# Decode attention with 256 MB of K and 256 MB of V on one core: tiles of 4 MB become tiles of 8 MB, and the sums of K's products move from ScalarE to GpSimd and VectorE

## The chip, the core and the metric

The kernel runs on one core of a Trainium2 chip. The core has TensorE (PE, matmuls), VectorE (DVE), ScalarE (ACT), GpSimd (POOL) and SyncE (SP, which here only issues transfers), and 16 DMA engines that move data between the chip's memory and the core's own memory of 128 partitions. The metric is the device time of one execution in microseconds.

## The reference

One decode step for two sequences (B = 2, one new token each, D = 512): a pre-normalised attention block over a cache of 8192 positions with 32 heads of width 128, and then a channel MLP with its own layer norms (F = 1792). All in float32. Cut to what matters:

```python
q = (layernorm(x) @ wq)                      # (2, 512) @ (512, 4096) -> 32 heads of 128
scores = einsum("bhqd,bhkd->bhqk", q, k_cache) * 128 ** -0.5     # k_cache: (2, 32, 8192, 128)
p = softmax(scores)
o = einsum("bhqk,bhkd->bhqd", p, v_cache)
h = x + o.reshape(2, 1, 4096) @ wo           # wo: (4096, 512)
y = layernorm(layernorm(h))
h2 = h + gelu(y @ w1 + b1) @ w2 + b2         # w1: (512, 1792), w2: (1792, 512)
```

k_cache and v_cache are 268 MB each (2 x 32 x 8192 x 128 x 4 bytes), wq and wo 8.4 MB each, w1 and w2 3.7 MB each. Everything is read once.

## The kernel before, in words

**Tiles.** A "pair" in this kernel is one head of one sequence; there are 64, in the order head 0 sequence 0, head 0 sequence 1, head 1 sequence 0, and so on. K of a pair is 8192 x 128 floats, 4 MB, and comes as one transfer into a tile of 128 partitions: partition p holds 64 positions in a row, so each partition receives one run of 32 KB. V comes in the same way. K, V, the two halves of wq, w1 and w2 share one pool of five slots of 4 MB (`kv`, `bufs=BUFS`). SP issues the transfers in the written order: in turn i the loop (L337 to L386) issues K of pair i + 1 and V of pair i - 1 (`load`, L204 to L209). An issue waits on SP until its slot is free, that is until the tile that held the slot has been used up.

**Scores.** q is made once (L175 to L184), kept in `q2`, and spread over all partitions in PSUM for two heads at a time (`make_q`, L188). For each of the two halves of a K tile VectorE multiplies the half by q in place (`multiply`, L217: 32 positions x 128). Then the products are summed over the 128 columns. ScalarE sums 10 of the 32 positions of a half, one instruction each with its accumulator read (`by_act`, L222), and VectorE the other 22 in one reduction (`by_dve`, L226). 

**Softmax.** After both sequences of a head, the maximum over all positions is found (`row_max` on VectorE, two transposes on TensorE, `all_max` on VectorE and a matmul that spreads it), and ScalarE takes the exponentials into a tile `ptz` that is zero elsewhere (`exps`, L250). `total` sums them with a matmul, `inverse` takes the reciprocal.

**Values.** For V, TensorE multiplies four positions per partition at a time (`values`, L271: 16 matmul groups per tile, 128 x 512 each, into `so2`). ScalarE copies the result out (`gather`), TensorE adds the parts (`head_sum`), VectorE scales by the inverse sum (`head_out`).

**wo.** The first 28 heads are multiplied by wo in four groups. Outputs are collected in a row layout `orow`, transposed per group (`turn`), and multiplied with the group's wo tile (`turned`, L326). The first two groups (7 heads each) get their wo through 24 small transfers that GpSimd issues (`load_spread`, L97 to L119), each after the last and with 16 tiny `fill` transfers between them; the other groups and the last four heads are loaded by SP. Most of wo comes in runs of 8 KB.

**Tail.** After the loop SP issues the last V in three pieces, then w1 in four and w2 in six (L388 to L395). The mean over D, the layer norm, w1, GELU and w2 follow (L397 to L494). The result leaves in two transfers of 2 KB, one on SP's queue and one on ScalarE's (L494). b1 and b2 are loaded by SP eight pairs before the end (L351 to L353).

**Order.** A scheduler places the instructions of each engine from the order in which the program writes them; `tc.issue_after` (`behind`, L331) ties a block of instructions behind a given one on the same engine. It also puts in the waits between engines, for reads after writes and for writes after writes, transfers among them.

Of the kernel before, what the change touches and what calls it, by code (L numbers as in the profile page):

```python
# [15 lines left out]
P = 128  # L16
EPS = 1e-5
QG = 2
WG = 8
LH = 4  # L20
UH = 7
SHUT = (0, 32)
CH = 32
NACT = 10
BUFS = 5
NG = 4
WARM = 3


@with_exitstack  # L30
def tile_decode_block(ctx: ExitStack, tc: tile.TileContext, x, k, v, wq, wo, w1, b1, w2, b2, out):
# [4 lines left out]
    NS = SK // P  # L36
    NC = NS // CH
# [3 lines left out]
    SCALE = DH ** -0.5  # L41

    const = ctx.enter_context(tc.tile_pool(name="const", bufs=1))
    wts = ctx.enter_context(tc.tile_pool(name="wts", bufs=1))
    wtl = ctx.enter_context(tc.tile_pool(name="wtl", bufs=1))
    kv = ctx.enter_context(tc.tile_pool(name="kv", bufs=BUFS))
    work = ctx.enter_context(tc.tile_pool(name="work", bufs=3))
# [3 lines left out]

    x2 = const.tile([B, D], F32, name="x2")
    nc.scalar.dma_start(x2, x.rearrange("b s d -> (b s) d"))

    wo_g = {}
    HL = H - LH

    NP7 = P - 8 * len(SHUT)
    groups = [[(0, UH, 0)], [(UH, UH, 0)], [(14, 2, 0), (16, 4, 2)], [(20, 4, 0), (24, 4, 4)]]
    spread_groups = 2
    part_of = {h: (g, pt) for g, parts in enumerate(groups) for pt in parts for h in range(pt[0], pt[0] + pt[1])}
    group_end = {parts[-1][0] + parts[-1][1] - 1: g for g, parts in enumerate(groups)}
    group_rows = [WG if g < spread_groups else sum(pt[1] for pt in parts) for g, parts in enumerate(groups)]

    def load_wo(g):
        t = wts.tile([P, WG, D], F32, name="wog")  # L70
        for h0, n, r0 in groups[g]:
            nc.sync.dma_start(t[:, r0:r0 + n], wo[h0 * DH:(h0 + n) * DH, :].rearrange("(p r) n -> p r n", r=n))
        wo_g[g] = t

    wqv = wq.rearrange("(p r) n -> p r n", r=DC)
    wqs = []
    for r in range(0, DC, 2):
        t = kv.tile([P, 2, H * DH], F32, name="wqs", tag="kv")
        nc.sync.dma_start(t, wqv[:, r:r + 2, :])  # L79
        wqs += [t[:, 0, :], t[:, 1, :]]  # L80
# [3 lines left out]
    orow = const.tile([B, WG, P], F32, name="orow")  # L84
    nc.gpsimd.memset(orow, 0.0)
    fill = const.tile([2, 8, 2, 2], F32, name="fill")
    turns = iter(range(8 * spread_groups))
    pool = [nc.gpsimd.memset(fill, 0.0)]

    def in_turn(dst, src):  # L90
        with tc.issue_after(pool[0].ins):
            pool[0] = nc.gpsimd.dma_start(dst, src)  # L92

    def turn_to(n):
        in_turn(fill[:n, next(turns) % 8, :, 0:1], b1[:8 * n].rearrange("(p x a c) -> p x a c", p=n, x=2, a=2)[:, 0, :, 0:1])

    def load_spread(g, gate):  # L97
        t = wts.tile([P, WG, D], F32, name="wog")
        h0, n, _ = groups[g][0]
        with tc.issue_after(pool[0].ins):  # L100
            pool[0] = nc.gpsimd.tensor_copy(fill[:1, 0, 0, 1:2], gate)
        for p0 in SHUT:
            with tc.issue_after(pool[0].ins):
                pool[0] = nc.gpsimd.memset(t[p0:p0 + 8], 0.0)  # L104
        dst = t.rearrange("p (s r) n -> p s (r n)", s=2)
        src = wo[h0 * DH:(h0 + n) * DH, :].rearrange("(s q r) n -> q s (r n)", s=2, q=NP7)

        def piece(p0, k):
            q0 = p0 - sum(8 for x in SHUT if p0 > x)
            in_turn(dst[p0:p0 + 4 * k - 3:4], src[q0:q0 + 4 * k - 3:4])  # L110

        for j in range(4):
            turn_to(2)
            piece(40 + j, 14)
        for j in range(4):
            turn_to(2)
            piece(8 + j, 6)
            piece(96 + j, 8)
        wo_g[g] = t  # L119
# [319 lines left out]
    with behind(last):  # L439
        head_sum(hl)  # L440
# [80 lines left out]
```

## Time and profile before

| | |
|---|---|
| device time, median of 3 runs (lowest to highest) | 1317.86 us (1317.77 to 1317.9) |
| the profiled execution, first to last instruction | 1316.0 us |
| busy: VectorE, PE, ScalarE, GpSimd | 990.2, 521.9, 442.0, 39.0 us |
| moved by DMA | 561.65 MB, 427 GB/s over the span |
| of it through SP's and ScalarE's queues | 557.35 MB |
| through GpSimd's queue | 3.68 MB |

The runs report a time of their own; no separate total is given for the profiled execution, so its span is what sums are made against, and 1.9 us lie between it and the median of the runs. Lines of a profile read as follows. A group of instructions is "line engine operation output<-input shapes xcount | busy us, mean ns of one | idle time of the engine just before them <-what ended most of it". A stretch is "from:to, its length, busy us of PE, PEld, VectorE, ScalarE and GpSimd with counts, the granted TensorE clock, the share of the DMA engines' time, GB/s". A line in order of time is "start us, duration us, engine, line, operation". SPq and ACTq are the queues on which SP and ScalarE issue transfers; the duration there is that of the issue, not of the transfer. A line of waits is "engine line <- whom it waited for: total us, times, longest us". DMA issues are "what, queue, count, KB each, median us from issue to landing".

### The profile page before, as it was taken

To read this page: it belongs to the slowest core of one execution; us is meant where nothing else is said; L and a number is where in the kernel's file an instruction comes from. 1 tells how busy PE (TensorE), PEld (TensorE's weight loads), DVE (VectorE), ACT (ScalarE), POOL (GpSimd) and SP (SyncE) were. 2 spreads that over 40 slices of the span, in tenths; PEclk is the share of its full clock that TensorE was granted. 3 is DMA by queue.
4 is the path that set the end of the run, shared out by engine and by line. 5 is a ranking of instruction groups with operands and counts; after the bars stand their busy time and mean duration, and the time that the engine had idled before them with its cause. 6 is when DMAs were issued, how large, how long until landed. Compare 5 with 4: busy or idle time off the path is not lost.

```text
span 1316.0 us, 9726 instructions
## 1 busy us (share of the span) xinstructions
PE 521.9 (40%) x2906; PEld 142.2 (11%) x2907; DVE 990.2 (75%) x462; ACT 442.0 (34%) x2763; POOL 39.0 (3%) x58
## 2 busy tenths in 40 slices
PE   3043254234534243243543344262343432345347
PEld 1010011101101010011100001010010100011013
DVE  1998778778868778778768778778678778688771
ACT  0433334324323334334323333323233333243341
POOL 0310000000320000000000000000000000000000
PEclk9565766666776675666756766676666665767669
DMA  9999999999999999999999999999999999999997
GB/s 409 426 432 429 432 431 431 429 432 431 431 426 430 431 433 430 430 430 430 431 430 430 430 431 432 430 430 429 432 429 430 432 432 426 432 430 432 429 426 318
DMA packets 23597, 561.65 MB, mean 427 GB/s; under 512 B 3620, under 2 KB 3636, under 8 KB 5432
## 3 DMA queue, kind: packets, MB, share of 16 engines
q1 hardware_dynamic: 21868, 557.35, 98.8%
q0 software_dynamic: 1664, 3.68, 0.7%
q8 instruction: 23, 0.38, 0.1%
q14 instruction: 30, 0.25, 0.0%
q10 hardware_dynamic: 12, 0.01, 0.0%
HBM read 561.01 MB, written 0.00 MB: 426 GB/s over the span
## 4 chain that ended last, share of the span: by engine, by line
DMA 72%; DVE 20%; PE 6%; issue 1%; ACT 0%; SPq 0%; DVEq 0%
DMA kv<-in_A_k_cache_dram 53%; DMA kv<-in_A_v_cache_dram 15%; DVE kv L217 12%; DVE s L226 7%; PE so L271 4%; DMA w1s<-in_B_w_dram 3%; PE rowacc L326 1%; DMA w2s<-in_B_w_dram 1%; PE qps L192 0%; SPq L208 0%; DVE gm L240 0%; DVE orow L312 0%; ACT kv L222 0%; ACT L250 0%; SPq L79 0%
## 5 line engine op out<-in xcount | busy, mean ns | idle before, releaser
L217 DVE TENSOR_TENSOR kv<-kv,qps 128x4096 f32<-128x4096 f32 x128 | 562.2, 4413 | 275.9 <-DMA kv<-in_A_k_cache_dram 275.9
L222 ACT ACTIVATE kv<-kv 128x128 f32<-128x128 f32 x1280 | 376.0, 295 | 672.9 <-DVE kv L217 657.3
L271 PE MATMUL so<-kv,pt 128*8 128x512 f32 x2048 | 362.1, 847 | 201.9 <-DMA kv<-in_A_v_cache_dram 199.4
L226 DVE TENSOR_REDUCE s<-kv 128x22 f32<-128x2816 f32 x128 | 391.0, 3075 | 0.1
L222 ACT ACTIVATION_READ_ACCUMULATOR kv<-kv 128x1 f32 x1280 | 238.7, 187 | 0.0
L271 PEld LDWEIGHTS so<-kv,pt 128*8 128x8 f32 x2048 | 62.1, 113 | 444.3 <-issue 250.8
L242 PE MATMUL sm<-gm,srow 1*128 1x2 f32 x64 | 18.3, 354 | 193.2 <-DVE gm L240 193.2
L192 PE MATMUL qps<-q,pick 2*128 2x256 f32 x64 | 31.0, 634 | 151.2 <-DVE kv L217 151.2
L278 ACT ACTIVATE ss<-so 128x512 f32<-128x512 f32 x32 | 19.1, 597 | 155.0 <-PE so L271 155.0
L236 PE MATMUL sm<-ident,mx 128*1 128x128 f32 x64 | 17.9, 280 | 110.5 <-DVE mx L233 105.3
L242 PEld LDWEIGHTS sm<-gm,srow 1*128 1x128 f32 x64 | 15.7, 302 | 205.4 <-DVE gm L240 180.4
L259 PE MATMUL sm<-ones,ls 128*2 128x1 f32 x56 | 5.4, 165 | 75.4 <-ACT pt L250 75.4
L192 PEld LDWEIGHTS qps<-q,pick 2*128 2x128 f32 x64 | 17.6, 302 | 157.5 <-DVE kv L217 153.8
L326 PE MATMUL rowacc<-wog,ot 128*2 128x512 f32 x60 | 33.0, 713 | 3.7 <-issue 2.0
L288 PE MATMUL sm<-ss,sel 128*2 128x128 f32 x224 | 29.0, 273 | 13.8 <-ACT ss L278 13.7
L236 PEld LDWEIGHTS sm<-ident,mx 128*1 128x1 f32 x64 | 5.1, 79 | 165.9 <-DVE mx L233 138.3
L250 ACT ACTIVATE pt<-s,nb 128x64 f32<-128x64 f32 x64 | 21.7, 340 | 1.1
L288 PEld LDWEIGHTS sm<-ss,sel 128*2 128x2 f32 x224 | 16.7, 84 | 25.4 <-ACT ss L278 21.3
L233 DVE TENSOR_REDUCE mx<-s 128x1 f32<-128x64 f32 x64 | 14.0, 219 | 6.5 <-ACT kv L222 0.2
L180 PE MATMUL so<-wqs,yT 128*2 128x512 f32 x64 | 10.1, 789 | 11.9 <-DMA wqs<-in_A_wq_dram 11.9
L92 POOL DMA_DIRECT2D wog<-in_A_wo_dram x24 | 13.4, 558 | 40.3 <-DMA wog<-in_A_wo_dram 26.2
L104 POOL MEMSET wog<- 8x4096 f32 x4 | 14.0, 3502 | 5.4 <-PE rowacc L326 5.3
(91 smaller groups left out, 134.0 us busy)
## 6 DMA issues: line engine op xcount, KB each, us to landing
kv<-in_A_k_cache_dram SPq DMA_DIRECT2D x63, 4096.0 KB, 42.4
kv<-in_A_v_cache_dram SPq DMA_DIRECT2D x62, 4096.0 KB, 33.8
wqs<-in_A_wq_dram SPq DMA_DIRECT2D x2, 4096.0 KB, 12.0
kv<-in_A_v_cache_dram SPq DMA_DIRECT2D x3, 2048.0 KB
kv<-in_A_k_cache_dram SPq DMA_DIRECT2D x2, 2048.0 KB, 42.6
w1s<-in_B_w_dram SPq DMA_DIRECT2D x4, 896.0 KB, 33.8
wog<-in_A_wo_dram SPq DMA_DIRECT2D x3, 1024.0 KB, 39.6
w2s<-in_B_w_dram SPq DMA_DIRECT2D x2, 1024.0 KB
```

Source lines behind the costliest of these rows:

```text
L104: pool[0] = nc.gpsimd.memset(t[p0:p0 + 8], 0.0)
L192: nc.tensor.matmul(t[:, b], pick[32 * n:32 * n + B, b, :], q2[32 * n:32 * n + B, at:at + QG * DH], start=True, stop=True)
L217: return nc.vector.tensor_tensor(kc, kc, qb, op=ALU.mult)
L222: nc.scalar.activation(kt[:, j, :], kt[:, j, :], AF.Copy, accum_out=s[:, j:j + 1])
L226: nc.vector.tensor_reduce(ST[i][:, a:e], kt[:, a:e, :], axis=AX.X, op=ALU.add)
L236: nc.tensor.transpose(MT[h][:, e, :], MX[h][:, e:e + 1], ident)
L242: nc.tensor.matmul(GM[h], srow, gm, start=True, stop=True)
L250: nc.scalar.activation(ptz[h % 2][b][:, :, 4 * b:4 * b + 4], s.rearrange("p (u j) -> p u j", j=4), AF.Exp, bias=nb[:, b:b + 1], scale=SCAL ...
L271: m = nc.tensor.matmul(so[32 * n:32 * n + 4 * B], ptz[h % 2][b][:, u, :], vt[:, 4 * u:4 * u + 4, :], start=(b == 0 and u < NG), stop=(b == ...
L278: nc.scalar.activation(SS[h], so2[h % 2], AF.Copy)
L288: nc.tensor.matmul(OP[h], sel[:, :, j], sj, start=(j == 0), stop=(j == 3))
L326: nc.tensor.matmul(rowacc, t[:, r, :], wo_g[g][:, r, :], start=(g == 0 and r == 0), stop=False)
```

## The change

- **Tiles of 8 MB.** For heads 0 to 29, two heads of one sequence are loaded as one tile: head 2g in partitions 0 to 63, head 2g + 1 in partitions 64 to 127, 128 positions per partition, one run of 64 KB each. That makes 30 units (15 pairs of heads x 2 sequences). Heads 30 and 31 are a unit each, with both sequences in one tile, as two transfers (the last V as four) in runs of 32 KB or less. wq is one transfer of 8 MB. The pool has three slots of 64 KB per partition instead of five of 32. In turn i, V of unit i - 1 is issued first and K of unit i + 1 after it.
- **Sums.** A K tile has four parts of 32 positions. VectorE multiplies each. For the first three GpSimd adds the upper 64 columns of the products onto the lower 64 (`halve`), and VectorE sums 64 columns; the fourth it sums whole. ScalarE sums none. VectorE's written order is product 0, product 1, sum 0, product 2, sum 1, product 3, sum 2, sum 3.
- **One softmax per two heads.** Maxima, exponentials (four ScalarE instructions on 64 partitions each), totals, inverses, `values` and `gather` are done once per pair of heads and both sequences.
- **wo by pairs.** One transfer of 512 KB in runs of 4 KB per pair of heads, on SP; one for heads 30 and 31. `load_spread`, its `fill` transfers and all of GpSimd's DMAs are gone.
- **Small transfers.** In the eighth last unit 15 transfers of 1 to 15 short rows each are written into one unused tile `mark`, on SP, each over the one before. b1 and b2 are loaded after the last V, into the slot that w1 and w2 also take.
- **One store.** The result rows stand 16 partitions apart and leave in one transfer on SP. For this the last matmuls are 32 columns wide instead of 2.

```diff
-CH = 32
-NACT = 10
-BUFS = 5
+CH = 32
+NCH = 4
 NG = 4
+LH = 2
+MARKS = 15
...
+    heads = [(2 * g, 2 * g + 1) for g in range(NP)] + [(h, h) for h in range(HL, H)]
+    units = [(g, b) for g in range(NP) for b in range(B)] + [(g, None) for g in range(NP, NP + LH)]
...
-    kv = ctx.enter_context(tc.tile_pool(name="kv", bufs=BUFS))
+    wts = ctx.enter_context(tc.tile_pool(name="wts", bufs=2))
+    kv = ctx.enter_context(tc.tile_pool(name="kv", bufs=3))
...
+    def slot():
+        return kv.tile([P, ROW], F32, name="kv", tag="kv")
...
+    wqt = slot()
+    nc.sync.dma_start(wqt, wq.rearrange("(p r) n -> p (r n)", r=DC))
...
+    def load(src, i, parts):
+        g, b = units[i]
+        h = heads[g][0]
+        t = slot()
+        if b is not None:
+            nc.sync.dma_start(t, src[b, h:h + 2].rearrange("h (p j) d -> (h p) (j d)", j=NS2))
+            return t
+        tv = t.rearrange("p (b j d) -> p b j d", b=B, d=DH)
+        for e in range(B):
+            for s0, n in parts[e]:
+                nc.sync.dma_start(tv[:, e, s0:s0 + n],
+                                  src[e, h].rearrange("(p j) d -> p j d", j=NS1)[:, s0:s0 + n])
+        return t
+
+    def load_wo(g):
+        t = wts.tile([P, 2, D], F32, name="wog", tag="wog")
+        h = heads[g][0]
+        if g < NP:
+            nc.sync.dma_start(t, wo[h * DH:(h + 2) * DH, :].rearrange("(p r) n -> p r n", r=2))
+        else:
+            nc.sync.dma_start(t, wo[h * DH:, :].rearrange("(h p) n -> p h n", p=P))
+        WO[g] = t
...
+    def multiply(i, c, t):
+        g, b = units[i]
+        b = c // 2 if b is None else b
+        kc = chunk(t, c)
+        return nc.vector.tensor_tensor(kc, kc, QP[g][:, b, None, :].to_broadcast([P, CH, DH]), op=ALU.mult)
+
+    def halve(c, t):
+        kc = chunk(t, c)
+        nc.gpsimd.tensor_tensor(kc[:, :, 0:HP], kc[:, :, 0:HP], kc[:, :, HP:DH], op=ALU.add)
+
+    def add_up(i, c, t, n):
+        nc.vector.tensor_reduce(S[i][:, c * CH:(c + 1) * CH], chunk(t, c)[:, :, 0:n], axis=AX.X, op=ALU.add)
...
-    def by_act(i, c, kt):
-        s = ST[i]
-        for j in range((c + 1) * CH - NACT, (c + 1) * CH):
-            nc.scalar.activation(kt[:, j, :], kt[:, j, :], AF.Copy, accum_out=s[:, j:j + 1])
-
-    def by_dve(i, c, kt):
-        a, e = c * CH, (c + 1) * CH - NACT
-        nc.vector.tensor_reduce(ST[i][:, a:e], kt[:, a:e, :], axis=AX.X, op=ALU.add)
...
+    def exps(g):
...
+            s = S.pop(2 * g + b).rearrange("p (u j) -> p u j", j=4)
+            for e in range(2):
+                q, m = slice(e * HP, (e + 1) * HP), 2 * b + e
+                nc.scalar.activation(ptz[b][q, :, 4 * m:4 * m + 4], s[q], AF.Exp, bias=nb[q, b:b + 1],
+                                     scale=SCALE, accum_out=lt4[q, m:m + 1])
...
+    whole = [[(0, NS1)], [(0, NS1)]]
+    KT, VT = {0: load(k, 0, whole)}, {}
+    first = None
+    for i, (g, b) in enumerate(units):
+        if i >= 1:
+            VT[i - 1] = load(v, i - 1, whole)
+        if i + 1 < NU:
+            KT[i + 1] = load(k, i + 1, whole)
+        if b == 0 or i == NU - 2:
+            load_wo(g)
+        if i == NU - 8 and MARKS:
+            mark = const.tile([16, 32], F32, name="mark")
+            for n in range(1, MARKS + 1):
+                nc.sync.dma_start(mark[:n, :n + 8], b1[:n * 32].rearrange("(p c) -> p c", p=n)[:, :n + 8])
...
+        for c in range(NCH):
+            with behind(first):
+                m = multiply(i, c, kt)
+            first = None
+            if c < NCH - 1:
+                halve(c, kt)
+            with behind(m):
+                if c == 0:
+                    if b != 1 and g >= 1:
+                        inverse(g - 1)
+                    if out_of >= 0:
+                        first = head_out(out_of)
+                        turn(out_of)
+                elif c == 1:
+                    if out_of >= 0:
+                        first = turned(out_of)
+                    if b != 0 and g < GL:
+                        make_q(g + 1)
+            if c >= 1:
+                add_up(i, c - 1, kt, HP)
+            if c == 2 and b == 0 and i >= 1 or c == 2 and i == NU - 2:
+                values(i - 1, VT.pop(i - 1))
+                gather(g - 1)
+                head_sum(g - 1)
...
+        add_up(i, NCH - 1, kt, DH)
+        row_max(i)
+        if b != 0:
+            first = all_max(g)
+            exps(g)
+            total(g)
+        if b == 1:
+            values(i - 1, VT.pop(i - 1))
...
+    vlast = load(v, NU - 1, [[(0, NS1)], [(0, 32), (32, NS1 - 40), (NS1 - 8, 8)]])
+    wt = slot()
...
+    nc.gpsimd.memset(b1r, 0.0)
+    for e in range(B):
+        nc.sync.dma_start(b1r[16 * e::32], b1.rearrange("(n f) -> n f", n=NG))
+    for e in range(B):
+        nc.sync.dma_start(b2s[e:e + 1], b2[None, :])
...
-    for b, eng in zip(range(B), (nc.sync, nc.scalar)):
-        eng.dma_start(out[b].rearrange("s (n d) -> (s n) d", n=NG), res[b::32])
+    nc.sync.dma_start(out.rearrange("b s (n d) -> n (b s) d", n=NG), res[0:P:16])
```

More of the change, by code (lines that the diff above doesn't have):

```diff
@@ L66, in tile_decode_block @@
[L66 to L76, printed above, removed]
@@ L87, in tile_decode_block @@
[L87 to L119, printed above, removed]
```

451 lines of the change are left out of this document (197 added, 254 removed).

## The prediction

> **What bounds the kernel now.** I read the page's shares and slices first, then the chain that ended last, the waits of SP's queue, the costly groups, the stretches, and last the tail in order of time.
>
> ```profile
> span 1316.0 us, 9726 instructions
> PE 521.9 (40%) x2906; PEld 142.2 (11%) x2907; DVE 990.2 (75%) x462; ACT 442.0 (34%) x2763; POOL 39.0 (3%) x58
> ...
> DMA  9999999999999999999999999999999999999997
> GB/s 409 426 432 429 432 431 431 429 432 431 431 426 430 431 433 430 430 430 430 431 430 430 430 431 432 430 430 429 432 429 430 432 432 426 432 430 432 429 426 318
> ...
> q1 hardware_dynamic: 21868, 557.35, 98.8%
> q0 software_dynamic: 1664, 3.68, 0.7%
> q8 instruction: 23, 0.38, 0.1%
> q14 instruction: 30, 0.25, 0.0%
> ...
> DMA 72%; DVE 20%; PE 6%; issue 1%; ACT 0%; SPq 0%; DVEq 0%
> ```
>
> VectorE is busy for 75% of the span, but the 16 DMA engines are at 9 tenths or more in 39 slices of 40, at 426 to 433 GB/s after the start. The chain's DVE 20% is no bound by itself: it is the way from a landed K tile to the issue that refills its slot, and the transfers go on meanwhile. So the kernel takes the time of its 561 MB, plus the start, plus what follows the last byte. An edit helps only if it shortens the stream, or the ends; it hurts if it lets the stream run dry.
>
> ```profile
> SPq L208 <- DVE s L226: 1091.0, 63, 19.8
> ```
>
> SP waits 1091 us in all for VectorE to give K tiles back. That isn't lost, because a tile's issue comes long before its transfer begins:
>
> ```profile
> kv<-in_A_k_cache_dram SPq DMA_DIRECT2D x63, 4096.0 KB, 42.4
> ...
> w1s<-in_B_w_dram SPq DMA_DIRECT2D x4, 896.0 KB, 33.8
> ```
>
> 4 MB at 432 GB/s take 9.7 us, yet a K tile lands 42.4 us after its issue: three others stood before it.
>
> **What the DMA rate depends on.** Stretches of one kind of transfer (columns: stretch, length, busy time of PE, PEld, DVE, ACT, POOL, clock, DMA share, GB/s):
>
> ```profile
> 1.00:2.00 1.00, 0.00 (x0) 0.00 (x0) 0.95 (x6) 0.65 (x1) 0.96 (x2) 1.00 1.19 332
> 5.00:30.00 25.00, 12.65 (x76) 3.66 (x76) 0.90 (x6) 1.19 (x2) 0.00 (x0) 0.93 1.00 430
> 80.00:120.00 40.00, 18.58 (x103) 5.08 (x95) 34.07 (x15) 13.54 (x86) 3.92 (x7) 0.71 0.99 423
> 200.00:240.00 40.00, 14.01 (x78) 3.31 (x78) 31.79 (x15) 14.58 (x94) 0.00 (x0) 0.67 1.00 432
> 360.00:400.00 40.00, 12.55 (x78) 3.12 (x78) 29.06 (x14) 12.53 (x80) 9.77 (x18) 0.67 1.00 425
> 1296.00:1298.00 2.00, 1.59 (x11) 1.51 (x11) 0.16 (x1) 0.10 (x1) 0.00 (x0) 1.00 1.01 418
> 1306.00:1308.00 2.00, 1.06 (x32) 0.74 (x32) 0.65 (x1) 0.08 (x1) 0.00 (x0) 1.00 0.70 284
> 1308.00:1310.00 2.00, 1.60 (x48) 1.05 (x48) 0.00 (x0) 0.00 (x0) 0.00 (x0) 1.00 0.57 226
> 1310.00:1312.00 2.00, 1.09 (x28) 0.42 (x24) 0.00 (x0) 0.00 (x0) 0.00 (x0) 1.00 0.28 100
> ```
>
> K and V tiles move in 32 KB runs (4096 KB over 128 partitions) at 432 GB/s; w1 moves in 7 KB runs (896 KB over 128) at 418. One of 16 engines thus spends 16 x 32768 / 432 = 1213.6 ns on the long run and 16 x 7168 / 418 = 274.4 ns on the short one: 36.7 ns per KB (of 1000 bytes) and a fixed 11.4 ns per run. A 64 KB run should take 2415.8 ns, 434 GB/s.
>
> **The change part by part.**
>
> *Runs of 64 KB.* 60 of the 64 tiles of 8 MB (15 pairs, two batches, K and V) and wq, 61 in all, come in 64 KB runs; the last two heads stay at 32 KB. Each engine saves one fixed cost in each of 8 runs per tile: 61 x 8 x 11.4 ns = **-5.6 us**. Bounds: 0, if a 64 KB run is cut in two; -7, if the 418 of that short stretch was held down by 0.25% more. I take the fit, as both ends of it are plain stretches. wq lies in rows of 64 KB already (four rows of 16 KB a partition) and with K0 beside it runs at 430, so the wider spacing costs nothing. The Trainium skill ("DMA: Bandwidth & Descriptors", "Why small descriptors are slow (HBM only)") gives about 3 bus cycles of 32 bytes per packet on trn2; by that the saving would be 3 of 2051 cycles, an estimated 1.7 us, and the sum 3.9 us later. The trace's own difference, 418 against 432, is larger than that rule's, so I stay with the rows.
>
> *wo by pairs.* 26 heads whose wo came in 8 KB runs now come in 4 KB runs: 26 x 32 runs more, over 16 engines, 52 x 11.4 ns = +0.6 us; two heads go from 2 KB to 4 KB, -0.2 us. **+0.4 us.**
>
> *No DMAs from GpSimd.* The 40 transfers of the software queue go. The two stretches that hold most of them ran at 423 and 425 against 432: 40 x 9/432 + 40 x 7/432 = 1.5 us, of which 0.25 is their shorter runs, counted above. **-1.2 us** (0 to -1.5).
>
> *ScalarE sums nothing.*
>
> ```profile
> L222 ACT ACTIVATE kv<-kv 128x128 f32<-128x128 f32 x1280 | 376.0, 295 | 672.9 <-DVE kv L217 657.3
> L222 ACT ACTIVATION_READ_ACCUMULATOR kv<-kv 128x1 f32 x1280 | 238.7, 187 | 0.0
> L217 DVE TENSOR_TENSOR kv<-kv,qps 128x4096 f32<-128x4096 f32 x128 | 562.2, 4413 | 275.9 <-DMA kv<-in_A_k_cache_dram 275.9
> L226 DVE TENSOR_REDUCE s<-kv 128x22 f32<-128x2816 f32 x128 | 391.0, 3075 | 0.1
> L233 DVE TENSOR_REDUCE mx<-s 128x1 f32<-128x64 f32 x64 | 14.0, 219 | 6.5 <-ACT kv L222 0.2
> L104 POOL MEMSET wog<- 8x4096 f32 x4 | 14.0, 3502 | 5.4 <-PE rowacc L326 5.3
> masks.py:199 POOL TENSOR_SCALAR_AFFINE_SELECT ident<-ident 128x128 f32<-128x128 f32 x1 | 0.3, 282 | 0.0
> L271 PE MATMUL so<-kv,pt 128*8 128x512 f32 x2048 | 362.1, 847 | 201.9 <-DMA kv<-in_A_v_cache_dram 199.4
> ```
>
> 2560 ScalarE instructions go. Their time was beside the transfers and is worth nothing, but code is fetched by the same DMA engines: 0.63 MB for 9726 instructions is 65 bytes each, so 0.16 MB fewer, **-0.4 us**.
>
> *VectorE and GpSimd, per K tile of 8 MB.* Four products of 4413 ns; a sum costs (3075 - 219) / (2816 - 64) = 1.04 ns per element, so three half sums (2048) take 2.28 each and the whole one (4096) 4.40: 28.9 us, against 4 x (4.41 + 3.08) = 30.0 now. Row maximum, output scaling and the rest: 1.6. GpSimd's halving adds 2048 + 2048 elements per partition; the trace has no two-input GpSimd operation. The memset gives 0.855 ns per element written, 1.75 us, as the lower end; 282 ns for 128 elements read once, times 16, doubled for two inputs, 9.0 as the upper. I take 4.5, that row's own pass, which also lies well inside both ends. Then in VectorE's order (product 0, product 1, sum 0, product 2, sum 1, ...) sum 0 finds its half done at 4.4 + 4.5 = 8.9, when product 1 ends: no wait, 30.5 us a tile. The Trainium skill ("GPSIMD Engine Reference", "Performance versus the Vector engine") gives 4497 ns for such an add of 2048 and says that GpSimd contends with VectorE where that reads two SBUF inputs; the products read one from PSUM. By it the sum stays.
>
> *Three slots of 8 MB for five of 4 MB.* A slot is refilled for the third tile after its own, which must be queued when two more have landed: 2 x 8.39 MB / 434 = 38.7 us. K: 30.5 to consume, 0.33 to issue and 1 until bytes move (wq, issued at 0.75, moves 332 GB/s between 1 and 2 us): 6.9 us to spare. V of the first batch waits for the pair's softmax: it lands 19.3 after its pair's second K, which needs about 32 with maxima and exponentials, then the matmuls of 8 MB, 11.4 us (362.1 / 64 = 5.7 for 4 MB now): 44 of 58. V of the second batch has more. **0.** If the spare is gone, each us beyond costs some 30 us over the 30 K tiles. A startup pause is covered too: wq as one transfer lands near 21, K0 and K1 stand queued until 60, and the slot of wq is free near 32.
>
> *The 15 small "mark" transfers* on SP, from the eighth last unit on. Each writes over the one before, so SP waits for that to land, and the next load stands behind it. Does the written order put one mark between two loads, or all 15 together?
>
> ```profile
> 1.52 0.43 DVE L144 MEMSET b1r<- 128x448 f32 x1
> ...
> 1120.85 0.68 DVE L409 TENSOR_REDUCE wsum<-wol 128x1 f32<-128x512 f32 x1
> ...
> 1121.00 0.33 SPq L208 DMA_DIRECT2D kv<-in_A_v_cache_dram  x1
> 1121.38 0.66 SPq L352 DMA_DIRECT2D b1r<-in_B_b_dram  x1
> ```
>
> b1r could have gone out from 2 us on; SP sent it at 1121, in its place: a load that waits for a slot isn't overtaken. VectorE ran wsum, which stands behind the whole loop, at 1120.85: work whose input is missing is overtaken. So I expect mark 1, a load, mark 2, a load, and so on through the last 14 loads; while a mark waits for the tile before it, a whole tile of 19.3 us is still under way, which hides it. **0**, up to the rival below.
>
> *Tail.* V's end, w1, w2 follow in the same order. b1 and b2 now go out there: 4 small transfers, issued while V's last 16 MB are under way, so at nothing.
>
> ```profile
> 1306.81 1.06 PE L489 MATMUL po<-w2s,fT 128*2 128x128 f32 x32 [1.74 <-DVE fT L486]
> ...
> 1312.05 0.40 PE L489 MATMUL po<-w2s,fT 128*2 128x128 f32 x8 [0.24 <-DMA w2s<-in_B_w_dram]
> 1312.52 0.29 DVE L492 COPY res<-po 128x128 f32<-128x128 f32 x1 [5.76 <-PE po L489]
> 1312.83 0.56 SPq L494 DMA_DIRECT2D out_dram<-res  x1
> 1312.84 0.62 ACTq L494 DMA_DIRECT2D out_dram<-res  x1
> ```
>
> The arithmetic is ready at 1306.8 and then follows w2's bytes, 5 us of cover for anything added before it. From 1306 the rate falls to 284, 226 and 100: the DMA engines run out one after another, 2 x (116 + 174 + 300) / 400 = 2.9 us of the mean engine idle, taking 400 as the rate before. Which ones lag can't be read from the rates; I leave the term at 0, bounds -2.5 and +3. One store on SP alone instead of two, the later of which is ScalarE's (0.62 against 0.56): **-0.3 us** (0 to -0.6).
>
> **Sum.** -5.6 + 0.4 - 1.2 - 0.4 - 0.3 = -7.1 us. On the profiled span of 1316.0 that gives 1308.9; the median of the runs, 1317.86, lies 1.9 above the span, and keeping that: **1310.8 us**, 0.5% faster. With the bounds, 1306 to 1315.
>
> **The rivals.**
>
> *The runs buy nothing.* If 64 KB runs are cut in two, or 432 is the limit of the engines whatever the run, the first term is 0: 1316.4. For it: no slice of the page is above 433. The Trainium skill ("DMA: Bandwidth & Descriptors", "Where 436 GB/s comes from") puts the ceiling at 435.2, and 434 would still fit under it. Against it: 418 for short runs.
>
> *The marks starve the stream.* x, issued at 0.76 on an idle queue, is used at 3.05, so a small round trip takes about 2.3 us, and 0.35 to issue.
>
> ```profile
> 0.76 0.56 ACTq L53 DMA_DIRECT2D x<-in_A_x_dram  x1
> ...
> 3.05 0.62 DVE L157 BATCH_NORM_STATS2 lnst<-x 2x6 f32<-2x512 f32 x1
> ```
>
> Mark 1 stands behind everything queued; once it lands, the rings are empty. Each further mark before the next load costs 2.65 us of idle DMA: from two in a row it costs, from three it eats the gain, and all 15 in a row, 14 x 2.65 = 37 us, give 1348. For it: the program writes them in a row. Against it: the order seen at 1121.
>
> *K's slots come back late.* At GpSimd's upper end of 9 us the sums wait for the halves: a tile takes 11.3 + 3 x 9 + 1.6 = 39.9 us, against 37.4 allowed, 2.5 x 30 = 75 us, 1386. It decides from a halving of 8.2 us. For it: no row shows GpSimd with two inputs, or beside VectorE at work. Against: 4.5 by the nearest row.
>
> **How the numbers follow.** Forecast 0.63 (1306 to 1315), no gain from runs 0.12, marks 0.13, late slots 0.12. A measurement tells about 0.2% from no change, 2.6 us. The second case is within that; the forecast's upper edge too, but nearly all of it is faster: faster 0.64, same 0.12, slower 0.24. The range goes from 1305 to 1322, which takes in the first two cases and the mild part of the others (up to four marks in a row, or slots late by 0.3 us), 0.8 in all.
>
> **What would show it.** The slices at 433 to 434 instead of 430 to 432 with half as many large packets; no dip near 80 and 360; a K tile's product, halves and sums within 31 us of its landing and SP issuing more than 5 us before the queue is empty; GpSimd's add near 4.5 us; one mark between two loads. The prediction is wrong if the slices stay at 431, if a hole in the DMA row stands in the last quarter (marks), or if VectorE's sums wait for GpSimd in every tile.

## The result and the profile after

The changed kernel takes 1317.57 us (median of 12 runs, 1315.35 to 1320.08) against 1317.78 (12 runs, 1317.69 to 1317.93): a ratio of 0.9999, 95% interval 0.999 to 1.0007. No change can be measured, where 1310.8 was forecast. New is the spread: 4.7 us from the shortest to the longest run, where the kernel before has 0.24. The two longest runs, 1320.08 us each, have the lowest granted clocks of the twelve, 0.640 and 0.641, and the two shortest 0.654 and 0.653, but one at 0.658 took 1318.03.

The profiled execution took 1316.34 us with a span of 1314.2, so 2.1 us lie around it. First the page of the changed kernel: span and busy time, the slices, the packets and the chain.

```profile
span 1314.2 us, 6813 instructions
PE 459.7 (35%) x2829; PEld 148.8 (11%) x2829; DVE 950.5 (72%) x426; ACT 52.3 (4%) x173; POOL 436.6 (33%) x108
...
DMA  9999999999999999999999999999999999999996
GB/s 415 431 447 409 430 437 435 425 437 431 439 433 423 432 439 428 433 433 431 435 431 431 437 431 433 433 435 427 435 431 429 439 426 436 435 431 432 421 425 266
DMA packets 14403, 561.46 MB, mean 427 GB/s; under 512 B 1809, under 2 KB 1825, under 8 KB 5157
...
q1 hardware_dynamic: 14368, 561.03, 99.1%
...
DMA 52%; DVE 28%; PE 13%; issue 3%; ACT 1%; POOL 1%; SPq 0%; DVEq 0%; ACTq 0%
```

ScalarE has 173 instructions instead of 2763, the software queue is gone, and there are 9,200 packets fewer. In the chain that ended last PE has 13%, where it had 6%. Two things stand out in the slices: the fourth is at 409, and the last at 266 against 318 before. So the transfers stop earlier while the span goes on. The stretches at the end of the changed kernel (columns as in the prediction, the last three are the granted clock, the DMA share and GB/s) show it:

```profile
1300.00:1302.00 2.00, 2.00 (x29) 0.86 (x33) 0.51 (x3) 0.02 (x1) 0.00 (x0) 0.66 0.94 372
1302.00:1304.00 2.00, 2.00 (x15) 0.47 (x11) 0.16 (x1) 1.72 (x3) 0.00 (x0) 0.50 0.52 204
1304.00:1306.00 2.00, 2.00 (x19) 0.50 (x11) 0.54 (x1) 0.00 (x0) 0.00 (x0) 0.98 0.13 49
1306.00:1308.00 2.00, 0.21 (x5) 0.12 (x8) 0.79 (x2) 0.97 (x1) 0.00 (x0) 1.00 0.00 0
```

Before, 100 GB/s still moved from 1310 to 1312. Now nothing moves from 1306 to 1308, and the arithmetic still has 5 us to go. By the packets' own records the last one of w2 ends at 1305.05, against 1311.55: the stream became 6.5 us shorter, of 6.8 forecast. The gain was made, and lost behind the stream. The timeline of the changed kernel tells where (start, length, engine, line, operation, and in brackets the idle time before it and what ended it):

```profile
1276.12 5.61 PE L260 MATMUL so<-kv,pt 128*8 128x512 f32 x32
...
1283.76 1.02 PE L303 MATMUL rowacc<-wog,ot 128*2 128x512 f32 x2 [0.25 <-DVE ot L287]
1286.95 0.64 PE L416 MATMUL sm<-ident,kv 2*128 2x2 f32 x4 [2.17 <-DVE kv L408]
1287.52 8.47 PE L260 MATMUL so<-kv,pt 128*8 128x512 f32 x64
...
1305.27 0.82 PE L434 MATMUL wp<-kv 128*128 128x512 bf16 x3
...
1307.88 3.26 PE L476 MATMUL po<-kv 128*32 128x128 f32 x112 [1.79 <-DVE kv L473]
1311.21 0.29 DVE L479 COPY kv<-po 128x128 f32<-128x128 f32 x1 [3.39 <-PE po L476]
1311.57 0.60 SPq L480 DMA_DIRECT2D out_dram<-kv  x1
```

Line 260 is `values`. Its 32 products of the last but one head stand behind the last softmax, at 1276. VectorE's `base` chain (x plus wo's outputs, less the mean) needs their result, the transposes of line 416 need `base`, and all 64 products of the last head stand behind those in TensorE's queue. They end at 1295.99. Before, the last of them ended at 1295.45, by this line of the kernel before:

```profile
1289.70 5.75 PE L271 MATMUL so<-kv,pt 128*8 128x512 f32 x48
```

The hidden row, what w2's products multiply, is ready at 1307.88 (1306.81 before), and w2's 112 products run in one go, with nothing left to wait for. Before, they ran in five groups, held up by w2's bytes to 1312.45. The end moved from 1312.45 to 1311.14 in this execution and by 0.2 us in the medians.

What the prediction expected of the loop came about, as the groups and the waits of SP and VectorE of the changed kernel show:

```profile
L183 DVE TENSOR_TENSOR kv<-kv,qps 128x4096 f32<-128x4096 f32 x128 | 563.7, 4406 | 303.7 <-DMA kv<-in_A_k_cache_dram 294.1
L187 POOL TENSOR_TENSOR kv<-kv 128x2048 f32<-128x2048 f32 x96 | 433.7, 4525 | 828.8 <-DVE kv L183 494.3
L190 DVE TENSOR_REDUCE s<-kv 128x32 f32<-128x2048 f32 (+1 forms) x128 | 356.7, 2806 | 5.9 <-POOL kv L187 5.5
```

```profile
SPq L158 <- DVE s L190: 770.9, 29, 38.3
SPq L321 <- DMA mark<-in_B_b_dram: 173.7, 14, 21.0
```

GpSimd halves in 4.525 us, VectorE's sums wait for it for 5.5 us in all, and the 14 waits for a mark end before the queue is empty: in the last quarter no slice but the very last is below 421, so the stream did not stop there.

### The profile page after: what moved, and what is told of

It reads as the page before. It is cut to its first block, busy times and chain, and to the rows that moved or that the text cites. A ratio compares the mean times of both kernels' runs of the same rounds, so it can differ in the third digit from the quotient of the medians.

```text
span 1314.2 us, 6813 instructions
## 1 busy us (share of the span) xinstructions
PE 459.7 (35%) x2829; PEld 148.8 (11%) x2829; DVE 950.5 (72%) x426; ACT 52.3 (4%) x173; POOL 436.6 (33%) x108
## 4 chain that ended last, share of the span: by engine, by line
DMA 52%; DVE 28%; PE 13%; issue 3%; ACT 1%; POOL 1%; SPq 0%; DVEq 0%; ACTq 0%
DMA kv<-in_A_k_cache_dram 33%; DMA mark<-in_B_b_dram 17%; DVE kv L183 15%; DVE s L190 11%; PE so L260 11%; DMA kv<-in_A_v_cache_dram 2%; POOL kv L187 1%; PE sm L211 1%; ACT pt L229 1%; DVE orow L282 1%; DVE gm L207 0%; PE sm L202 0%; PE so L453 0%; DVE mx L200 0%; PE po L476 0%
## 5 line engine op out<-in xcount | busy, mean ns | idle before, releaser
L187 POOL TENSOR_TENSOR kv<-kv 128x2048 f32<-128x2048 f32 x96 | 433.7, 4525 | 828.8 <-DVE kv L183 494.3
L260 PE MATMUL so<-kv,pt 128*16 128x512 f32 (+1 forms) x2048 | 305.5, 734 | 275.6 <-DMA kv<-in_A_v_cache_dram 255.0
L190 DVE TENSOR_REDUCE s<-kv 128x32 f32<-128x2048 f32 (+1 forms) x128 | 356.7, 2806 | 5.9 <-POOL kv L187 5.5
L260 PEld LDWEIGHTS so<-kv,pt 128*16 128x16 f32 (+1 forms) x2048 | 77.2, 111 | 468.2 <-DMA kv<-in_A_v_cache_dram 270.6
L292 PE MATMUL sm<-bmask,orow 4*128 4x2 f32 x60 | 15.1, 352 | 190.5 <-DVE orow L282 190.5
L147 PE MATMUL qps<-q,pick 2*64 2x128 f32 x136 | 18.0, 411 | 150.5 <-DVE kv L183 150.5
L299 PE MATMUL rowacc<-wog,ot 128*2 128x512 f32 x60 | 53.0, 1037 | 49.6 <-DVE ot L296 49.6
L292 PEld LDWEIGHTS sm<-bmask,orow 4*128 4x128 f32 x60 | 13.8, 317 | 193.3 <-DVE orow L282 178.8
L229 ACT ACTIVATE pt<-s,nb 64x128 f32<-64x128 f32 x60 | 23.9, 399 | 1.2
L274 PE MATMUL sm<-ss,sel 128*4 128x128 f32 x120 | 15.6, 273 | 10.9 <-ACT ss L266 10.9
```

Source lines behind the costliest of these rows:

```text
L147: nc.tensor.matmul(QP[g][s * HP:(s + 1) * HP, b], pick[32 * n:32 * n + B, b, :], q2[32 * n:32 * n + B, at:at + DH], start=True, stop=True)
L187: nc.gpsimd.tensor_tensor(kc[:, :, 0:HP], kc[:, :, 0:HP], kc[:, :, HP:DH], op=ALU.add)
L190: nc.vector.tensor_reduce(S[i][:, c * CH:(c + 1) * CH], chunk(t, c)[:, :, 0:n], axis=AX.X, op=ALU.add)
L229: nc.scalar.activation(ptz[b][q, :, 4 * m:4 * m + 4], s[q], AF.Exp, bias=nb[q, b:b + 1], scale=SCALE, accum_out=lt4[q, m:m + 1])
L260: m = nc.tensor.matmul(so[32 * n:32 * n + w], p[:, u, cols], t[:, (at + u) * 512:(at + u + 1) * 512], start=(b == 0 and u < NG), stop=(b = ...
L274: nc.tensor.matmul(OP[g], sel4[:, :, j], sj, start=(j == 0), stop=(j == 3))
```

## The experiments

All medians are in us; the kernel before measured 1317.82 to 1317.84 beside each of them.

**How much cover the end had.** Two runs lay some 2.6 us on the last piece of arithmetic, one in each kernel.

```diff
-    nc.vector.transpose(fT, ff)
+    for _ in range(5):
+        nc.vector.transpose(fT, ff)
```

In the changed kernel:

> The changed kernel with the last transpose of the hidden row done five times instead of once, which lays 4 x 0.65 = 2.6 us on the arithmetic ahead of w2's products and on nothing else. Theory (the arithmetic sets the end, w2's bytes have long landed): +2.6 us, near 1320.2, all of w2's products still in one go. Rival (the end is set by w2's bytes or the engines that lag): +0 to 0.3, 1317.6 to 1317.9.

In the kernel before:

> The kernel before with the last transpose of the hidden row done five times, 2.6 us more on the same piece of arithmetic. Theory (there w2's bytes set the end, and the arithmetic has 5 us of cover): +0 to 0.5 us, 1317.8 to 1318.3. Rival (the cover told in the prediction was never there): +2.6, 1320.4.

Measured: 1321.26 (1320.75 to 1324.23) in the changed kernel, 3.7 more; 1321.27 (1319.58 to 1321.96) in the kernel before, 3.45 more. The first bears the theory out in sign and is 1.1 us too large. The second contradicts what I expected: the arithmetic of the kernel before did not have 5 us of cover. The timeline of the kernel before with the delay, and its stretches, show why:

```profile
1306.85 3.36 DVE L487 STREAM_TRANSPOSE fT<-ff 128x448 f32<-128x448 f32 x5 [1.03 <-ACT ff L484]
1310.26 4.75 PE L490 MATMUL po<-w2s,fT 128*2 128x128 f32 x112 [4.46 <-DVE fT L487]
```

```profile
1308.00:1310.00 2.00, 0.00 (x0) 0.00 (x0) 1.90 (x4) 0.00 (x0) 0.00 (x0) 1.00 0.59 234
1310.00:1312.00 2.00, 1.74 (x36) 1.22 (x40) 0.21 (x1) 0.00 (x0) 0.00 (x0) 0.50 0.23 85
1312.00:1314.00 2.00, 2.00 (x56) 1.48 (x52) 0.00 (x0) 0.00 (x0) 0.00 (x0) 0.65 0.00 0
```

Two parts were missing from the 5 us. w2's 112 products themselves take 3.26 us once the hidden row is there, as the changed kernel's timeline has it; they ended at 1312.45 before, so the row could come at 1309.19 at the latest: 2.4 us of cover. And TensorE, idle for 4.46 us, got half the clock for the products: 4.75 us instead of 3.26. In this execution the row came 1.07 us after 1309.19 and the products took 1.49 longer, 2.56 together; it took 1320.39, 2.57 more than the kernel before. In the changed kernel the same happened without any cover:

```profile
1310.62 4.93 PE L477 MATMUL po<-kv 128*32 128x128 f32 x112 [4.51 <-DVE kv L474]
```

The row came 2.74 us later than without the delay and the products took 1.67 longer, 4.41 together, where the two profiled executions lie 4.45 apart. That is why the delay cost more than its length there.

**Whether the idle time halves the clock.** The same delay in the kernel before, with 10 and then 18 more small products in front of w2's to keep TensorE busy.

```diff
-        keep_warm(WARM)
+        keep_warm(WARM + 10)
```

> The kernel before with the last transpose of the hidden row done five times, as in the run with 1321.27 us, and 13 instead of 3 small products that keep TensorE busy in front of w2's. Theory (of the 3.45 us that the delay cost there, more than half was TensorE's clock, which had fallen to half in the idle time, so that w2's 112 products took 4.75 us and not 3.3): the products take 3.3 to 3.6 us again, span 1317.0 to 1317.6, time near 1319. Rival (the delay alone, by its length, ends the kernel later): unchanged, 1321 to 1321.5. Second rival (5 us of cover, as the prediction had it, with the clock as the only cost): 1317.8.

Measured: 1320.83 (1317.84 to 1321.14), which is a little under the first rival's 1321 to 1321.5. One of the ten runs took no longer than the kernel before, and nothing shows why. In the profiled execution:

```profile
1305.26 2.98 PE L446 MATMUL wp<-wb 128*128 128x512 bf16 x13
...
1310.55 4.91 PE L490 MATMUL po<-w2s,fT 128*2 128x128 f32 x112 [2.31 <-DVE fT L487]
```

The products still took 4.91 us, at 0.50 from 1312 to 1314. The theory as put there failed. But the 13 small products ended at 1308.24 and w2's began at 1310.55, so TensorE was idle for 2.31 us of the 3.4 us before the clock fell (the trace's record has it at half from 1311.4 to 1314.8). The second run fills that gap:

```diff
-        keep_warm(WARM)
+        keep_warm(WARM + 18)
```

> The kernel before with the last transpose of the hidden row done five times, and 21 small products in front of w2's, so that TensorE is idle for about half a us before them and not for 2.3 us as with 13 of them. Theory (a stretch of 3.4 us in which TensorE is mostly idle is followed by one at half clock, and 13 products still left one such stretch; of the delay itself only what goes past the cover of 2.3 us counts): w2's 112 products take 3.3 to 3.6 us, time 1318.8 to 1319.4. Rival (the stretches at half clock come whatever TensorE does): the products take 4.7 to 4.9 us, 1320.8 to 1321.3.

Measured: 1319.18 (1318.0 to 1319.66). The timeline and a stretch of this run:

```profile
1304.69 4.71 PE L446 MATMUL wp<-wb 128*128 128x512 bf16 x21
...
1309.98 3.24 PE L490 MATMUL po<-w2s,fT 128*2 128x128 f32 x112 [0.58 <-DVE fT L487]
```

```profile
1312.00:1314.00 2.00, 1.22 (x47) 0.89 (x36) 0.29 (x1) 0.00 (x0) 0.00 (x0) 1.00 0.00 0
```

Full clock, 3.24 us, 1.34 us over the kernel before. By the medians the delay costs 3.45 us with the idle time that it makes and 1.34 without it, so some 2.1 are the idle time; in the profiled executions the products took 1.5 to 1.65 longer at half the clock. The cover of 2.4 us holds in the other two as well: the row came 1.36 and 0.79 us after 1309.19, and with the products' own 1.65 and 0 that is 3.0 and 0.8, where these executions took 3.0 and 0.9 more than the kernel before. The five transposes took 2.7 us more than the one (3.36 against 0.65), so 0.3 would be left of it behind the cover. It was more, because they also began later (at 1306.56 to 1307.13 in the three profiled executions, at 1306.11 before), and nothing hides such a lateness once the cover is gone; what makes up the rest of the 1.34 was not followed up. The Trainium skill ("TensorE: Matmul & The Clock Gate", "What's actually happening") says that the clock is set by how busy TensorE was in windows of 3413 ns that run on by themselves, half after an idle one. These runs agree as to the windows: the steps in the trace's clock record come 3.41 us apart or a multiple of it. How much idleness is enough they don't show; in the changed kernel the clock fell at 1300.7 too, behind a window of which TensorE spent 2.6 us on small products of two columns.

**Whether TensorE's order at the end is the cause.** The first of the two runs takes both moves, the second only that of the last head.

```diff
         add_up(i, NCH - 1, kt, DH)
-        row_max(i)
+        with behind(values(i - 1, VT.pop(i - 1), 1) if i == NU - 1 else None):
+            row_max(i)
...
-    values(NU - 2, VT.pop(NU - 2), 1)
...
-    for c in range(DC):
-        nc.tensor.transpose(bcp[:, c, :], basec.rearrange("b (p c) -> b c p", c=DC)[:, c, :], ident[:B, :B])
+    with behind(values(NU - 1, vlast, 0)):
+        for c in range(DC):
+            nc.tensor.transpose(bcp[:, c, :], basec.rearrange("b (p c) -> b c p", c=DC)[:, c, :], ident[:B, :B])
...
-    values(NU - 1, vlast, 0)
     last = values(NU - 1, vlast, 1)
```

> The changed kernel with TensorE's order altered at the end alone: the values of the second batch of the last but one head stand ahead of the last softmax's transposes, the values of the first batch of the last head ahead of the transposes of base. Theory (the stream is 6.5 us shorter as forecast, and the arithmetic behind the last V, held up in TensorE's queue, took its place as the end): V's last rows land near 1287.7 and are consumed within 1.5 us, the transposed hidden row is ready near 1300 and waits for w2, whose last byte lands near 1305; span 1309.5, time near 1311.5, and the runs lie within 0.5 us of one another again. First rival (the end is set by the DMA engines that run out last, or by the store, whatever TensorE does): unchanged, 1317.6 with a spread of some 4 us. Second rival (it is TensorE's lower clock at the end that makes the arithmetic long, the order only moves the same work): 1 to 3 us faster, 1315 to 1316.5.

> The changed kernel with only the second of the two moves at the end: the values of the last head's first batch stand ahead of the transposes of base, the rest of TensorE's order is as in the changed kernel. Theory (what holds up the end is the 8.5 us of values after V's last rows, because the base chain of VectorE stands ahead of them in TensorE's queue): the first batch's 4 us of values run from about 1283, the second's end near 1291.5 against 1295.9, the hidden row near 1303.5, span 1310 to 1311, time 1312 to 1313. Rival (the late values of the last but one head, behind the last softmax, are what counts): unchanged, 1317.6, or less than 2 us faster.

Measured: 1311.88 with both (1310.76 to 1311.92; ratio to the kernel before 0.9953, 0.994 to 0.9965), 1312.48 with the second alone (1312.38 to 1314.53; 0.9965, 0.9952 to 0.9977). The timeline of the run with both:

```profile
1269.17 5.32 PE L260 MATMUL so<-kv,pt 128*8 128x512 f32 x32 [4.21 <-DMA kv<-in_A_v_cache_dram]
...
1280.80 5.51 PE L260 MATMUL so<-kv,pt 128*8 128x512 f32 x29
1286.23 0.64 PE L417 MATMUL sm<-ident,kv 2*128 2x2 f32 x4
1286.80 3.62 PE L260 MATMUL so<-kv,pt 128*8 128x512 f32 x32
...
1301.93 2.48 PE L476 MATMUL po<-kv 128*32 128x128 f32 x80 [1.81 <-DVE kv L473]
1304.99 1.09 PE L476 MATMUL po<-kv 128*32 128x128 f32 x24 [0.59 <-DMA kv<-in_B_w_dram]
1306.30 0.43 PE L476 MATMUL po<-kv 128*32 128x128 f32 x8 [0.22 <-DMA kv<-in_B_w_dram]
1306.80 0.29 DVE L479 COPY kv<-po 128x128 f32<-128x128 f32 x1 [4.92 <-PE po L476]
```

The last head's values end at 1290.4 instead of 1296.0, the hidden row is ready at 1301.9, and w2's products wait for bytes again. The same work in another order takes 5.7 us less and brings the forecast time to within 1.1 us. The second move alone gives 5.1 of them by the medians, though two of its five runs, at 1314.33 and 1314.53, gave only about 3. There the products again ran in one go, from 1303.83, so the end still hung on the arithmetic. The rival by which the end hangs on the engines that run out last is refuted: nothing of the transfers was touched. So is the one that puts all of it down to the clock, for 1 to 3 us. The products that stand behind the `base` chain are now 32 in 3.62 us and not 64 in 8.47, and at the rate of these 32 the 64 would still take 7.2. By an estimate from these rows the clock gave 1.2 us there and 0.4 at w1's products (4.5 us against 5.0), where the hidden row came 5.9 us earlier. The spread shrinks to 1.2 us, which fits an end that no longer hangs on TensorE's clock; that the 4.7 us of the changed kernel come from there was only argued.

**What the runs of 64 KB are worth.** The kernel with both moves, with each tile and wq in two halves by columns.

```diff
...
-            nc.sync.dma_start(t, src[b, h:h + 2].rearrange("h (p j) d -> (h p) (j d)", j=NS2))
+            for s in range(2):
+                nc.sync.dma_start(t[:, s * ROW // 2:(s + 1) * ROW // 2],
+                                  src[b, h:h + 2].rearrange("h (p j) d -> (h p) (j d)", j=NS2)[:, s * ROW // 2:(s + 1) * ROW // 2])
```

> The kernel with the altered end order (the run before this one), with each 8 MB tile and wq brought by two transfers of half the columns each, so in 32 KB runs again; tiles, slots and arithmetic stay. Theory (a run has a fixed cost of 11.4 ns): 61 x 8 x 11.4 ns = 5.6 us slower than the kernel with the altered end, so near 1317; large packets near 1215 ns against 2420. Rival (the runs buy nothing, the stream got shorter because GpSimd's transfers and ScalarE's instructions went): within 0.7 us of the kernel with the altered end. Second rival (rate is bounded elsewhere, so only part of it counts): 2 to 4 us slower.

Measured: 1314.36 (1314.26 to 1314.56), 2.5 more and not 5.6, which is what the second rival gives. A whole account of the stream tells why. For a time t, it gives t less the bytes moved until then divided by 432 GB/s: how many us the stream lies behind a constant rate of 432. It is worked out from the packets of the queues that carry data.

```
   t    before   changed   both moves   32 KB runs   first tile halved
   98    2.88     2.23        2.29         2.64           2.40
  110    3.00     3.26        3.44         2.64           2.45
  200    3.49     3.25        3.60         3.01           2.34
 1250    8.54     2.87        3.16         6.49           1.99
 1300    9.60     4.36        4.75         7.85           3.57
packet of 32 KB: median 1216 ns before, 1215 with 32 KB runs
packet of 64 KB: median 2420 ns in the changed kernel
```

From 200 to 1250 the runs of 32 KB lose 3.5 us on 432, the runs of 64 KB gain 0.4. But the two kernels here whose first tile of 8 MB comes in one piece lose 1.0 and 1.2 us between 98 and 110, and the two with halves do not. That is the slice with 409. Some of what the 32 KB runs cost is hidden by this hole, which they don't have. SP's timeline of the changed kernel:

```profile
32.20 0.33 SPq L158 DMA_DIRECT2D kv<-in_A_v_cache_dram  x1
70.85 0.33 SPq L158 DMA_DIRECT2D kv<-in_A_k_cache_dram  x1
99.48 0.33 SPq L158 DMA_DIRECT2D kv<-in_A_v_cache_dram  x1
```

and VectorE's:

```profile
42.06 8.75 DVE L183 TENSOR_TENSOR kv<-kv,qps 128x4096 f32<-128x4096 f32 x2 [35.56 <-DMA kv<-in_A_k_cache_dram]
```

The first product waits for the whole 8 MB, to 42.06. With 28.7 us for each of the first two K tiles, the slot of the second comes free at 99.4, and by then the third K tile, the last one queued, has nearly landed. So one more run halves the first K tile alone.

```diff
...
-    KT, VT = {0: load(k, 0, whole)}, {}
+    KT, VT = {0: load(k, 0, 2)}, {}
...
```

> The kernel with the altered end order, with the first K tile alone brought by two transfers of half the columns. Theory (the stream runs dry for about 1.1 us near 100 us, because the first K tile is used only when all 8 MB of it have landed, at 42 us, and the slot for the second V tile comes free 30 us after the second K tile's turn): the first product starts near 32, SP issues the second V tile near 92 instead of 99.4, no hole near 100, and with 8 runs of 10 ns more per engine the time is 1.0 us lower: near 1310.9. Rival (the hole is made up for later, since other waits are behind it): unchanged, 1311.9.

Measured: 1310.17 (1309.91 to 1310.25), ratio to the kernel before 0.9941, 0.9929 to 0.9954: the best of these kernels but for the one without the small transfers, from which it can't be told apart. SP sends the second V tile earlier:

```profile
64.07 0.33 SPq L160 DMA_DIRECT2D kv<-in_A_k_cache_dram  x1
93.02 0.33 SPq L160 DMA_DIRECT2D kv<-in_A_v_cache_dram  x1
```

The hole is gone. Of the 1.7 us, 1.2 stand in the account; the other 0.5 is within the spread of the run with both moves. Set against this run, which also starts without a hole, the 32 KB runs cost 4.2 us for 480 runs more per engine: 8.7 ns each.

**GpSimd's spare.** An addition of zero ahead of each halving, in the kernel with both moves.

```diff
...
+        nc.gpsimd.tensor_tensor(kc[:, :, 0:HP], kc[:, :, 0:HP], nil[:, :, None].to_broadcast([P, CH, HP]), op=ALU.add)
         nc.gpsimd.tensor_tensor(kc[:, :, 0:HP], kc[:, :, 0:HP], kc[:, :, HP:DH], op=ALU.add)
```

> The kernel with the altered end order, with an addition of zero of the same size ahead of each of GpSimd's halvings, so that GpSimd takes 9.05 us per quarter tile. The result stays. Theory (6.9 us of spare in a K tile's round, and the halvings one after another set it from 8.2 us on): a K tile takes 4.4 + 3 x 9.05 + 2.3 + 4.4 + 0.3, 38.6, to 39.9 us against 37.4 that the slots allow: 1.2 to 2.5 us for each of 30 tiles, 1348 to 1387, with VectorE's sums waiting for GpSimd in every tile. Rival (the spare is larger than worked out, or V's slots give way): below 1320.

Measured: 1341.14 (the mean of 1338.48 and 1343.79). The groups, the waits and two stretches of this run:

```profile
L190 POOL TENSOR_TENSOR kv<-kv,nil 128x2048 f32<-128x2048 f32 x96 | 345.4, 3598 | 508.9 <-DVE kv L186 306.2
L191 POOL TENSOR_TENSOR kv<-kv 128x2048 f32<-128x2048 f32 x96 | 433.9, 4520 | 7.5
```

```profile
DVE s L194 <- POOL kv L191: 164.3, 81, 5.8
```

```profile
96.00:110.00 14.00, 1.12 (x8) 0.75 (x8) 10.92 (x5) 0.00 (x0) 10.61 (x3) 0.50 0.21 89
...
200.00:1200.00 1000.00, 345.91 (x2047) 107.80 (x2036) 792.23 (x305) 33.37 (x121) 616.19 (x153) 0.65 1.00 430
```

The addition took 3.6 us, not 4.5, so GpSimd needed 8.12 us a quarter, just below the 8.2 from which the prediction let it decide. The sums wait in 81 of 96 cases, and yet the stream keeps 430 GB/s from 200 to 1200: by the account some 5 us are lost there, and 14.5 at the start, where 89 GB/s moved from 96 to 110; the rest, 7 us of this execution, lies at the end and was not followed up. Neither theory foresaw 1341. The loop's small loss at 8.12 agrees with a threshold of 8.2, but no run goes past it; the place that breaks first is the start.

**The small transfers and the store.** Without the 15 marks, first with both moves, then with the halved first tile:

```diff
-MARKS = 15
+MARKS = 0
```

> The kernel with the altered end order, without the 15 small transfers. Theory (they cost nothing, one stands between two loads): 1311.9, within 0.4. Rival (each holds SP's queue up for something): 0.5 to 3 us faster. Second rival (they shift which DMA engine takes which piece of the last loads, so that the engines run out more evenly): up to 2 us slower without them.

> The kernel with the altered end order and the first K tile in two transfers, without the 15 small transfers. Theory (the 0.6 us that they made before lies within the spread of those runs): 1310.0 to 1310.3. Rival (they cost 0.5 us on SP's queue or on the engines): 1309.6.

Measured: 1311.25 (1310.5 to 1311.74) against 1311.88 with them, and 1310.04 (1309.81 to 1310.44) against 1310.17. Both lie within the spreads: the marks cost nothing that can be told, although the page of the changed kernel puts 17% of the chain that ended last down to them (DMA mark<-in_B_b_dram 17%). A share of that chain is not a price.

With the halved first tile, and two stores:

```diff
-    nc.sync.dma_start(out.rearrange("b s (n d) -> n (b s) d", n=NG), res[0:P:16])
+    for b, eng in ((0, nc.sync), (1, nc.scalar)):
+        eng.dma_start(out[b].rearrange("s (n d) -> (s n) d", n=NG), res[16 * b::32])
```

> The kernel with the altered end order and the first K tile in two transfers, with the result stored by two transfers again, one on SP and one on ScalarE. Theory: 0.3 us slower (0 to 0.6), near 1310.5. Rival (the end of the span does not hang on the store's issue): unchanged, 1310.2.

Measured: 1310.33 (1310.28 to 1310.56), 0.16 more, with no overlap of the runs: about half of what was expected.

## Why the prediction was wrong, point by point

**The step that failed** is in the tail: "The arithmetic is ready at 1306.8 and then follows w2's bytes, 5 us of cover for anything added before it." Three things in it were wrong. The cover was 2.4 us, since w2's products take 3.26 us after the hidden row, and the three profiled executions with the delay in the kernel before come out by it to 0.1 us. The change took 6.5 us off the bytes, so the cover was used up by the gain itself, even if nothing was added; I counted it as if both ends moved together. And the arithmetic did not come earlier with V, because its order on TensorE ties all of the last head's values to the base chain, and that to the last softmax. Altering that order alone gave 5.7 us back. The sum of the terms was a sum for the stream; the last step, that the end follows the stream, was not worked out for the new order. It could have been: the row of the last V products in the kernel before (5.75 us for 48, ending at 1295.45) and the order in the code were there.

**Runs of 64 KB**, forecast -5.6: -4.2 by the times of two kernels that differ in nothing else but the runs of all tiles after the first and of wq, 8.7 ns a run instead of 11.4; the medians of the packets give 2 x 1215 - 2420 = 10. The forecast's sign of it, slices at 433 to 434, can't be read from the page, where they lie between 421 and 439 from the fifth to the last but one; over 200 to 1250 us the rate is 432 against 430. The bound of -7 doesn't follow from its condition: a rate 0.25% below 418 would make 12.3 ns a run and -6.0. The rival that they buy nothing is refuted; that its time of 1316.4 is near the measured one is an accident. The rule of the Trainium skill that the prediction set beside the term ("DMA: Bandwidth & Descriptors", "Why small descriptors are slow (HBM only)": about three cycles a packet, by which it estimated 1.7 us) gives too little by these runs.

**GpSimd's DMAs, the shorter code and wo by pairs**, forecast -1.2 together: the account at 1250 has 8.54 before and 6.49 with the same 32 KB runs, so -2.05, of which 0.24 stand at the start already (2.88 and 2.64 at 98). These three weren't taken apart. In wo's +0.4 the two heads that go from 2 KB to 4 KB are 8 runs an engine, -0.1 and not -0.2.

**The slots**, forecast 0: right in the loop, wrong at the start. "A startup pause is covered too" looked at wq's slot and the first two K tiles, and not at the second V tile, which waits for the slot of the second K tile: 1.0 to 1.2 us, and 0.9 of it are still there at 1250 (2.87 against 1.99).

**GpSimd's 4.5 us, the sums without a wait, one mark between two loads**: as forecast (4.525 us; 5.5 us of waits in all; 0 within the spread). That the 4.5 fits is in part luck, as the row it was taken from is another operation with one input. **One store**, forecast -0.3: -0.16. **The skew of the engines at the end**, left at 0 within -2.5 and +3: the lead is 5.2 us at 1300 (9.60 against 4.36) and 6.5 at w2's last byte, so -1.3. By the account the runs' -4.5 at 1250 (6.49 and 1.99), the -2.05 and the slots' +0.9 make the lead of 5.7 there; 0.4 of it is lost until 1300, and the last 1.3 bring it to 6.5. The forecast of -6.8 for the stream was right as a sum, with its terms wrong by about 1 us each way: that they cancel is luck.

**The chances.** The time lies within the range, but not for a reason that the range was made of: no rival of the prediction came about. The case that did, a stream that gets shorter while the arithmetic behind it does not, was not among them; a rival that names what ends last after the gain would have been worth more than the one on the marks.

## What to carry to other kernels

When an edit shortens the resource that sets the end, work out anew what else ends near there: the cover of the next chain is its slack, less all that it still has to do after its last input, and a gain larger than that slack is lost from that point on. An in-order queue at the end deserves the same look as the loop: work whose data are there shouldn't stand behind a chain that needs another engine. A larger tile costs at the start of a stream, because the first use waits for the whole of it, so the first one is worth splitting.

## What the runs showed of the hardware

A delay in front of the last products can cost more than its length: 2.7 us of waiting became 3.45 to 3.7 by the medians. In the profiled executions TensorE was granted half its clock after 2.3 to 4.5 us of idleness (112 products in 4.75 to 4.93 us against 3.24 to 3.26), and with 21 small products that kept it busy it was not, which took 2.1 us of the 3.45 away. An addition on GpSimd whose second input is one element read again and again took 3.60 us where two full inputs took 4.52.
